# Layout of the first token step's result: 256 adjacent moving elements for the second step, in a state-space convolution kernel

## Chip, cores and metric

The kernel runs on one core of a Trainium2 chip, in one launch. The metric is the time of one execution on the device, in microseconds (us). Three runs of the kernel before gave 220.14, 220.74 and 221.19 us; their median, 220.74 us, is the time before. One more execution was profiled; it took 220.31 us, and its span from the first to the last instruction is 218.5 us.

## What is computed

The reference normalises the input rows, convolves every channel with a long kernel built from the state-space parameters (by FFT over 4096 points), gates the result with a small routed feed-forward network, and adds it to the input:

```
xn = layernorm(A_u)                                   # [1, 2048, 512]
dt = exp(log_dt)
P  = exp(dt * (A_re + i A_im) * l),  l = 0..2047
K  = real(sum_n C[d, n] * P[d, n, l] * dt * B[d, n])  # [512, 2048]
y  = irfft(rfft(pad(xn^T)) * rfft(pad(K)))[:2048]^T + xn * Dskip
r  = xn @ w_r;  row i = argmax(r)
moe = xn, with y_i * sigmoid(r_i) added to row i,
      y_i = (silu(xn_i @ w_gate) * (xn_i @ w_up)) @ w_down
out = A_u + y * silu(moe)
```

The operands are bfloat16.

## The kernel before, in words

The transform over tokens is done with matmuls, in two steps for the input and again for the kernel's spectrum and the way back. The program first writes down a graph of some 925 operations; each carries the SBUF bytes and PSUM banks that it reads and writes, and from these the semaphore waits are derived (`_Graph.op`, `emit`). The order on each engine is a table written out by hand (`ORDER`, applied in `schedule`). Every engine executes its list in order: an instruction that waits holds up all that stands behind it on its engine. The table also fixes which of the PSUM copies run on ScalarE and which on VectorE (`evac`, lines 614 and 615). SyncE's list (SP) holds nearly all DMA issues, so a DMA whose wait is not over holds up the DMAs behind it.

The stages around the change, in the order of time:

- **Norm and router** (`norm`, `new`, `nap`, `nmv`, `rt`, `rarg`). X0 and the parameters' staging tile STG lie in SBUF region RA; the normalised rows XN are moved by DMA into XZN, so that 32 partitions by four quarters hold the tokens.
- **First token step** (`useq`): 16 blocks of four matmuls of 128x256 (moving operand CB's F1, 256 adjacent elements), each into a pair of PSUM banks of 1024 floats. One copy per block (`evac`) writes 1024 bfloat16 per partition into AU, which lies in RA over X0 and STG. ORDER puts 11 of the 16 copies on ScalarE, 5 on VectorE.
- **Second token step** (`useq2`): the table F2U comes by two DMAs into the space that XZN leaves. 16 blocks (one for each pair of frequencies k2) of eight matmuls: stationary operand F2U, 64 rows by 128 columns; moving operand 256 elements of AU on 64 partitions. Two matmuls with `tile_position` (0, 0) and (64, 0) work on the upper and the lower 64 rows of the array at the same time, and write to different PSUM banks; this is a pair below. Each block has four pairs, and alternates between two PSUM bank pairs. A copy on ScalarE takes each block's 1024 floats per partition into one of two UST buffers; after two blocks a buffer goes to DRAM (`scr_u`), from where `load_u` later fetches it, turned, as UU.
- **Beside the second step** ScalarE makes the sines (tile QQ, line 581) and VectorE the products from which the convolution kernel is built: `kgen_g` (tiles TT and GG) and `kgen_q` (QQ). In the table the copies UST stand between groups of four sine instructions. `kgen_mm`, `kgen_kx` (matmuls of QQ with GG, copies KE, KS, KX) turn them into the kernel's points; the small copy K2R on VectorE waits for KX. PE's list mixes the blocks of the second step with the matmuls of the routed network (weights in the ring WRING, vectors in SMB), whose middle is one ScalarE silu and one VectorE product on SMB.
- **Then** the spectrum (`spec`: table FD, loaded in four pieces over RA, that is over AU and WRING; copies KF; product UU), the way back (`inv_a`: copies C) and the last step with the gate (`fin`: TB, XR, stores).

Before the change AU is laid out `[64, 4, 32, 2]`: token group m, quarter a, frequency k2, real or imaginary. The two lines that the change turns around are 879, the copy, and 892, the moving operand:

```
evac(AU(AU.a[4 * m4:4 * m4 + 4].reshape(1024)), pair(pair.a))
lst.append((o_, F2U(...), AU(AU.a[:, :, k2, ri].transpose(1, 0), 64 * par, 64), ...
```

So each copy reads 1024 adjacent floats and writes 1024 adjacent bfloat16, while one moving operand is made of 64 elements 512 bytes apart, four times.

Of the kernel before, what the change touches and what calls it, by code (L numbers as in the profile page):

```python
# [10 lines left out]
BF16 = mybir.dt.bfloat16  # L11
# [398 lines left out]
def build(nc, A_u, A_A_re, A_A_im, A_B_re, A_B_im, A_C_re, A_C_im, A_log_dt, A_Dskip,  # L410
          B_x, B_w_r, B_w_gate, B_w_up, B_w_down, out):
    g = _Graph(nc)
# [54 lines left out]
    with g.ctx:  # L467
# [29 lines left out]
        RA = o + -o % 32  # L497
# [11 lines left out]
        def cb(nm):  # L509
            a, n = cbo[nm]  # L510
            return CB.a[a:a + n]
# [7 lines left out]
        X0 = g.buf("X0", RA, [16, 512], BF16)  # L519
        STG = g.buf("STG", RA + 16 * KB, [6, 4, 128], BF16)  # L520
        ST6 = g.buf("ST6", RA + 22 * KB, [16, 6], F32)
        AU = g.buf("AU", RA, [64, 4, 32, 2], BF16)
        WRING = [g.buf(f"WRING{i}", RA + 32 * KB + 1536 * i, [768], BF16) for i in range(5)]
        FD = g.buf("FD", RA, [32, 5, 128], BF16)
        XN = g.buf("XN", RB, [4, 2, 16, 64], BF16)
# [9 lines left out]
        F2U = g.buf("F2U", RC, [32, 192], BF16)  # L535
# [32 lines left out]
        def cost(eng, v, rate):  # L568
            return FIX[eng] + v.n * rate
# [43 lines left out]
        def evac(out, in_):  # L613
            g.op(AC, lambda e: e.activation(out=out.ap, in_=in_.ap, func=ACT.Copy), w=[out], r=[in_], cost=cost(AC, out, 0.834) - 43,  # L614
                 alt=(DV, lambda e: e.tensor_copy(out=out.ap, in_=in_.ap), cost(DV, out, 1.042)))  # L615
# [10 lines left out]
        def mm(lst, ns):  # L626


            def fn(e):
                for o_, l_, r_, st, sp, pos in lst:  # L630
                    kw = {} if pos is None else {"tile_position": pos}
                    if sp is None:
                        kw["skip_group_check"] = True
                        sp = True
                    ins = e.matmul(o_.ap, lhsT=l_.ap, rhs=r_.ap, start=st, stop=sp, **kw)  # L635
                return ins

            outs, rds, so, sr = [], [], set(), set()
            for o_, l_, r_, _, _, _ in lst:
                k = (o_.banks[0], o_.p0 // 32, (o_.p0 + o_.pn - 1) // 32)  # L640
                if k not in so:
                    so.add(k)
                    outs.append(o_)
                for x in (l_, r_):
                    k = (id(x.buf), x.p0, x.pn, x.idx.tobytes())
                    if k not in sr:
                        sr.add(k)
                        rds.append(x)
            g.op(PE, fn, w=outs, r=rds, cost=ns * len(lst))
# [8 lines left out]
        def store(dst, src, nbytes, eng=SP, tokr=(), tokw=(), w=()):  # L658
            dma(dst, src.ap, nbytes, w=w, r=[src], eng=eng, tokr=tokr, tokw=tokw)

        def dram(t, off, dims):
            return bass.AP(tensor=t, offset=off, ap=dims)
# [112 lines left out]
        for bp in range(8):  # L775
            g.stage = f"rt{bp // 4}"
            pr_, xt = PP[2 * (bp % 2)], XT[bp % 3]
            lst = []
# [51 lines left out]
        for dc in range(4):  # L830
            for wi in range(2):
                W = (B_w_gate, B_w_up)[wi]
                for hf, (f0, fn_) in enumerate(((0, 6), (6, 5))):
# [7 lines left out]
                    lst = [(mv(140, 32), CB(cb("IDB")), gu, True, False, None)] if first else []  # L841
                    for fc in range(f0, f0 + fn_):
                        Mf = 128 if fc < 10 else 96
                        o_ = 128 * (fc - f0)
# [31 lines left out]
        for m4 in range(16):  # L876
            pair = PP[1 + m4 % 2]
            mm([(pair(pair.a[256 * i:256 * i + 256]), XZN(XZN.a[:, :, 4 * m4 + i].reshape(128)), CB(cb("F1")), True, True, None) for i in range(4)], 107)
            evac(AU(AU.a[4 * m4:4 * m4 + 4].reshape(1024)), pair(pair.a))
        g.stage = "ldf2"  # L880
        for k in range(2):
            load(F2U(F2U.a[16 * k:16 * k + 16].reshape(-1)), t_f2u.ap()[:, 3072 * k:3072 * k + 3072], 128 * 6144)
# [1 line left out]
        for kp in range(16):  # L884
            pair = PP[1 + kp % 2]
            lst = []
            for kk in range(2):
                k2 = 2 * kp + kk
                for ri in range(2):
                    for par in range(2):  # L890
                        o_ = pair(pair.a.reshape(2, 4, 2, 2, 32)[par, :, :, kk])
                        lst.append((o_, F2U(F2U.a[k2, 64 - 64 * ri:192 - 64 * ri], 64 * par, 64), AU(AU.a[:, :, k2, ri].transpose(1, 0), 64 * par, 64),
                                    ri == 0, ri == 1, (64 * par, 0)))
            mm(lst, 50)
            st = UST[(kp // 2) % 2]
            j_ = 2 * (kp % 2)
            evac(st(st.a.reshape(2, 8, 128)[:, :, 32 * j_:32 * j_ + 64].transpose(1, 0, 2)), pair(pair.a.reshape(8, 2, 64)))
            if kp % 2:
                store(dram(SCRU, 256 * (kp // 2), [[16384, 128], [2048, 8], [1, 256]]), st(st.a.reshape(8, 256)), 128 * 4096, tokw=[f"scru{kp // 2}"])
# [280 lines left out]
def bass_recurrent_scan__ssm_conv_s4__moe_arch_mod__prompt_kernel(  # L1180
    nc: bass.Bass,
    A_u: bass.AP,
    A_A_re: bass.AP,
    A_A_im: bass.AP,
    A_B_re: bass.AP,
    A_B_im: bass.AP,
    A_C_re: bass.AP,
    A_C_im: bass.AP,
    A_log_dt: bass.AP,
    A_Dskip: bass.AP,  # L1190
    B_x: bass.AP,
    B_w_r: bass.AP,
    B_w_gate: bass.AP,
    B_w_up: bass.AP,
    B_w_down: bass.AP,
    out: bass.AP,
):
    build(nc, A_u, A_A_re, A_A_im, A_B_re, A_B_im, A_C_re, A_C_im, A_log_dt, A_Dskip,
          B_x, B_w_r, B_w_gate, B_w_up, B_w_down, out)
# [28 lines left out]
```

## Time and profile before

| | before |
|---|---|
| median of three runs | 220.74 us |
| the profiled execution | 220.31 us |
| its span | 218.5 us |
| PE busy (matmul) | 157.5 us, 72% |
| VectorE (DVE) busy | 176.9 us, 81% |
| ScalarE (ACT) busy | 143.1 us, 65% |
| mean granted TensorE clock | 0.823 |

Times in the profile are microseconds from the span's start, durations of one instruction are also given in nanoseconds. PE is the matmul, PEld the load of a stationary operand beside it, DVE is VectorE, ACT ScalarE, SPq SyncE's queue of DMA issues. `L614` is line 614. `AU,F2U` behind an arrow are the tiles that an instruction reads; `x128` counts instructions. A row of the timeline gives start, length, engine, line, operation, tiles and count, and in brackets how long the engine had been idle and whose end released it; a row may merge several instructions in a row. A row of groups gives busy time in us, the mean of one in ns, then the idle time before them with the releasers. PEclk is the share of TensorE's full clock that was granted. Matmuls are pipelined: the length of one is the time from its start until its result is there, so the pace of a row of matmuls is read from the distance of their starts. A wait for several semaphores is put down to the one that came last by the profile.

### The profile page before, as it was taken

The page shows a single profiled execution, that of the slowest core. Times are in us where ns is not written, and L with a number is a line of the kernel's source. Part 1 is how long each engine was busy: PE and PEld are TensorE (multiplying, and loading weights), DVE is VectorE, ACT ScalarE, POOL GpSimd, SP SyncE. Part 2 cuts the span into 40 slices and gives each one's busy share as a digit, 9 for nine tenths or more (in the row PEclk, how much of TensorE's full clock was granted, in tenths as well). Part 3 has the DMA queues.
Part 4 walks back from the last instruction along what each step waited for, and adds up shares of the span by engine and source line. Part 5 has one row for each costly group of instructions (what it writes and reads, how often), then busy time and mean ns, then how long its engine had stood idle before and what let it go on. Part 6 is the DMA issues. An engine that isn't in the chain of part 4 may idle for free.

```text
span 218.5 us, 6289 instructions
## 1 busy us (share of the span) xinstructions
PE 157.5 (72%) x2707; PEld 116.9 (54%) x2707; DVE 176.9 (81%) x371; ACT 143.1 (65%) x225; POOL 4.2 (2%) x8
## 2 busy tenths in 40 slices
PE   0300768276728799998988699799976999978650
PEld 0300656144622233632366489698975999967530
DVE  1799999969999479559579997899955799959882
ACT  3599999969995784234141352349947299887670
POOL 0000000001200000000000000300000000000000
PEclk9999997559975555585559999999999799997885
DMA  6920079980076746667289999149198599992577
GB/s 202 338 98 1 2 172 220 177 339 3 0 231 253 214 138 173 180 174 202 60 305 325 357 361 226 37 98 249 47 257 204 96 349 248 204 181 42 94 124 141
DMA packets 37567, 38.90 MB, mean 178 GB/s; under 512 B 10820, under 2 KB 29604, under 8 KB 37156
## 3 DMA queue, kind: packets, MB, share of 16 engines
q1 hardware_dynamic: 34836, 37.46, 64.9%
q10 hardware_dynamic: 2640, 1.04, 2.0%
q8 instruction: 21, 0.34, 0.7%
q14 instruction: 6, 0.05, 0.1%
q0 software_dynamic: 64, 0.00, 0.0%
HBM read 28.01 MB, written 8.39 MB: 167 GB/s over the span
## 4 chain that ended last, share of the span: by engine, by line
PE 56%; DVE 20%; ACT 8%; DMA 5%; issue 5%; SPq 4%; DVEq 0%
PE PB L635 56%; SPq L652 4%; DMA X<-in_A_u_dram 3%; DVE ST L729 3%; DMA XZN<-XN 2%; DVE XN L753 2%; ACT C L614 2%; DVE AU L615 2%; DVE TT L586 1%; ACT AU L614 1%; DVE XR L586 1%; DVE TB L586 1%; DVE UU L586 1%; DVE PAR L586 1%; ACT KF L614 1%
## 5 line engine op out<-in xcount | busy, mean ns | idle before, releaser
L635 PE MATMUL PB<-KX,FD 128*128 128x128 bf16 x640 | 40.4, 221 | 1.6 <-ACT KF L614 1.2
L635 PEld LDWEIGHTS PB<-KX,FD 128*128 128x128 bf16 x640 | 36.7, 99 | 6.1 <-issue 3.3
L635 PE MATMUL PB<-AU,F2U 64*128 64x256 bf16 x128 | 29.4, 602 | 6.3 <-DVE GG L586 4.6
L586 DVE TENSOR_TENSOR TT<-GG,MB 128x512 bf16<-128x512 bf16 (+4 forms) x48 | 30.3, 664 | 0.4
L614 ACT ACTIVATE C<-PB 64x512 bf16<-64x512 f32 x43 | 25.2, 591 | 6.9 <-PE PB L635 4.6
L614 ACT ACTIVATE KF<-PB 128x512 bf16<-128x512 f32 x26 | 15.3, 596 | 22.1 <-PE PB L635 18.4
L614 ACT ACTIVATE UST<-PB 128x1024 bf16<-128x1024 f32 x16 | 16.2, 1026 | 15.7 <-PE PB L635 15.7
L586 DVE TENSOR_TENSOR UU<-UU,KF 128x1024 bf16<-128x1024 bf16 x32 | 21.2, 684 | 5.1 <-ACT C L614 2.6
L635 PE MATMUL PB<-QQ,GG 128*24 128x32 bf16 x1024 | 21.4, 252 | 4.3 <-issue 3.5
L635 PE MATMUL PB<-CB,UU 128*128 128x128 bf16 x256 | 20.9, 240 | 4.1 <-issue 2.2
L635 PEld LDWEIGHTS PB<-QQ,GG 128*24 128x24 bf16 x1024 | 18.5, 134 | 7.4 <-issue 4.4
L635 PEld LDWEIGHTS PB<-CB,UU 128*128 128x128 bf16 x256 | 18.9, 152 | 5.1 <-issue 2.5
L635 PE MATMUL PB<-CB,XN 128*64 128x128 bf16 x128 | 7.5, 297 | 17.1 <-DVE XN L753 15.0
L615 DVE CAST C<-PB 64x512 bf16<-64x512 f32 x21 | 14.4, 687 | 6.1 <-PE PB L635 4.0
L586 DVE TENSOR_TENSOR GG<-TT 128x256 bf16<-128x256 bf16 (+4 forms) x48 | 17.9, 407 | 0.4
L581 ACT ACTIVATE QQ<-TH 128x512 bf16<-128x512 f32 x32 | 18.1, 630 | 0.0
L581 ACT ACTIVATE QQ<-AR 128x512 bf16<-128x512 f32 x33 | 18.1, 614 | 0.0
L635 PEld LDWEIGHTS PB<-AU,F2U 64*128 64x128 bf16 x128 | 6.7, 115 | 20.8 <-issue 13.7
L635 PEld LDWEIGHTS PB<-CB,XN 128*64 128x64 bf16 x128 | 6.1, 158 | 17.8 <-DVE XN L753 15.2
L635 PE MATMUL PB<-CB,XZN 128*128 128x256 bf16 x64 | 11.6, 323 | 5.1 <-DMA XZN<-XN 1.6
L729 DVE BATCH_NORM_STATS2 ST<-X 128x6 f32<-128x512 bf16 x16 | 10.3, 680 | 6.1 <-DMA X<-in_A_u_dram 6.1
L586 DVE TENSOR_TENSOR QQ<-QQ 128x2048 bf16<-128x2048 bf16 (+1 forms) x8 | 14.0, 1755 | 0.2
(120 smaller groups left out, 217.6 us busy)
## 6 DMA issues: line engine op xcount, KB each, us to landing
FD<-c_fd SPq DMA_DIRECT2D x4, 1280.0 KB, 8.6
scr_u<-UST SPq DMA_DIRECT2D x8, 512.0 KB, 4.1
UU<-scr_u SPq DMA_DIRECT2D x8, 512.0 KB, 8.0
UU<-scr_u SPq DMA_DIRECT2D x16, 256.0 KB, 7.6
X<-in_A_u_dram SPq DMA_DIRECT2D x4, 512.0 KB, 6.3
XZN<-XN SPq DMA_DIRECT2D x16, 128.0 KB, 4.1
scr_g<-XN SPq DMA_DIRECT2D x4, 512.0 KB, 7.4
G<-scr_g SPq DMA_DIRECT2D x2, 1024.0 KB
```

The source lines that it names most:

```text
L581: g.op(AC, lambda e: e.activation(out=out.ap, in_=in_.ap, func=func, **kw), w=[out], r=r, cost=cost(AC, out, 0.834) - (43 if in_.buf.space ...
L586: g.op(eng, lambda e: e.tensor_tensor(out=out.ap, in0=a.ap, in1=b.ap, op=op), w=[out], r=[a, b], cost=cost(eng, out, rate))
L614: g.op(AC, lambda e: e.activation(out=out.ap, in_=in_.ap, func=ACT.Copy), w=[out], r=[in_], cost=cost(AC, out, 0.834) - 43, alt=(DV, lambd ...
L615: alt=(DV, lambda e: e.tensor_copy(out=out.ap, in_=in_.ap), cost(DV, out, 1.042)))
L635: ins = e.matmul(o_.ap, lhsT=l_.ap, rhs=r_.ap, start=st, stop=sp, **kw)
L652: fn = lambda e: e.dma_start(dst, src)
L729: g.op(DV, lambda e, b=b: e.bn_stats(ST6(ST6.a[b]).ap, X0(X0.a[b]).ap), w=[ST6(ST6.a[b])], r=[X0(X0.a[b])], cost=620)
L753: lambda e, ov=ov, iv=iv, mv_=mv_, rv=rv: e.tensor_scalar(out=ov.ap, in0=iv.ap, scalar1=mv_.ap, scalar2=rv.ap, op0=ALU.subtract, op1=ALU.m ...
```

## The change

AU is laid out `[32, 2, 4, 64]`: frequency, real or imaginary, quarter, token group. The copy of block m4 now reads its 1024 floats in the order (frequency and part, quarter, i), that is with steps of 256 floats, 64 floats and 1 float, and writes 256 runs of 4 adjacent bfloat16 (8 bytes), 128 bytes apart. The moving operand of the second step is 256 adjacent elements. The number, engines and order of the instructions stay, and so do the computation and the bytes. Which bytes of RA each copy writes and each matmul reads is another, so the derived waits of two kinds differ: the first copies now touch all of AU's 32 KB, and a piece of FD overlays the AU of some k2 alone.

```
-        AU = g.buf("AU", RA, [64, 4, 32, 2], BF16)
+        AU = g.buf("AU", RA, [32, 2, 4, 64], BF16)
...
-            evac(AU(AU.a[4 * m4:4 * m4 + 4].reshape(1024)), pair(pair.a))
+            evac(AU(AU.a[:, :, :, 4 * m4:4 * m4 + 4].reshape(64, 4, 4)), pair(pair.a.reshape(4, 4, 64).transpose(2, 1, 0)))
...
-                        lst.append((o_, F2U(F2U.a[k2, 64 - 64 * ri:192 - 64 * ri], 64 * par, 64), AU(AU.a[:, :, k2, ri].transpose(1, 0), 64 * par, 64),
+                        lst.append((o_, F2U(F2U.a[k2, 64 - 64 * ri:192 - 64 * ri], 64 * par, 64), AU(AU.a[k2, ri].reshape(256), 64 * par, 64),
```

## Prediction

> **What bounds the kernel now.** I read the page first, then the stretches from 66 to 112 us in the timeline, and VectorE's waits there.
>
> ```profile
> PE 56%; DVE 20%; ACT 8%; DMA 5%; issue 5%; SPq 4%; DVEq 0%
> ...
> L635 PE MATMUL PB<-AU,F2U 64*128 64x256 bf16 x128 | 29.4, 602 | 6.3 <-DVE GG L586 4.6
> ```
>
> PE carries 56% of the chain that ended last, and the second token step, the 128 matmuls on AU, keeps PE busy for 29.4 us. What paces them shows in the timeline, where the matmuls of one block stand in one row:
>
> ```profile
> 66.58 1.89 PE L635 MATMUL PB<-AU,F2U 64*128 64x256 bf16 x8 [4.57 <-DVE GG L586]
> 76.89 3.61 PE L635 MATMUL PB<-AU,F2U 64*128 64x256 bf16 x16 [1.76 <-ACT UST L614]
> 92.09 5.34 PE L635 MATMUL PB<-AU,F2U 64*128 64x256 bf16 x24
> ...
> 83.30:86.60 3.30, 3.30 (x16) 0.50 0.72 199
> 93.60:96.90 3.30, 3.30 (x18) 1.00 0.73 198
> ...
> 44.55 1.95 PE L635 MATMUL PB<-CB,XZN 128*128 128x256 bf16 x8 [1.62 <-DMA XZN<-XN]
> 46.76 1.10 PE L635 MATMUL PB<-CB,XZN 128*128 128x256 bf16 x4 [0.26 <-ACT AU L614]
> 44.50:49.10 4.60, 3.84 (x16) 2.51 (x16) 0.50 0.86 354
> ```
>
> Eight more matmuls take 3.61 - 1.89 = 1.72 us, four pairs of 0.43 us; the tail behind the last pair is 1.89 - 4 x 0.43 = 0.17 us. The block of 24 runs at the same 0.43 us ((5.34 - 0.17)/12), though the granted clock, which the rows of stretches give behind the busy times, is 1.00 from 93.6 us and 0.50 around 85 us. So the pair is not paced by the array's clock. The first token step also moves 256 elements per matmul, adjacent ones: four more take 1.95 - 1.10 = 0.85 us, 0.21 us each, at a clock of 0.50. A pair on AU therefore takes just twice what its 256 columns need at the low clock, and the difference between the two operands is the order in memory.
>
> This alone doesn't say what it is worth: the matmuls stand between copies on ScalarE and products on VectorE. VectorE waits only three times between 66 and 112 us, and I take these as the accounts in which a gain must show:
>
> ```profile
> DVE SMB L586 <- ACT SMB L581: 4.5, 1, 4.5
> DVE TT L586 <- ACT QQ L581: 4.2, 1, 4.2
> DVE K2R L596 <- ACT KX L614: 3.9, 1, 3.9
> ...
> 110.70:120.00 9.30, 8.28 (x276) 6.64 (x280) 9.09 (x21) 2.27 (x4) 0.00 (x0) 0.82 0.94 316
> ```
>
> After the third, VectorE is busy for 9.09 of 9.30 us (the third busy time in the row): from there it is at work without a break, and what it starts earlier, it hands on.
>
> **The matmuls.** With adjacent elements I price a pair at 0.21 us, the low-clock row of the first step. A block then takes 4 x 0.21 = 0.85 us plus the tail, and saves 1.72 - 0.85 = 0.87 us. That both matmuls of a pair still run at once is not shown for row tiles with adjacent elements; the pairs of column tiles in the last step show two dense streams at once:
>
> ```profile
> 185.09 0.64 PE L635 MATMUL PB<-C,FB 128*64 128x128 bf16 x16
> 185.00:185.70 0.70, 0.70 (x20) 1.00 1.11 243
> 57.71 0.68 PE L635 MATMUL PB<-CB,XZN 128*128 128x256 bf16 x4 [0.32 <-ACT AU L614]
> 50.68 1.12 PE L635 MATMUL PB<-CB,XZN 128*128 128x256 bf16 x8 [0.56 <-DVE AU L615]
> ```
>
> 16 of them take 0.64 us with the tail; one after another, at the 0.11 us per 256 columns of the first step's faster rows ((1.12 - 0.68)/4), they would take 16 x 0.055 + 0.17 = 1.05 us. Bounds for a pair: 0.11 us, if the clock is full, and 0.43 us, if the pair doesn't overlap. I take 0.21 because the clock was at 0.50 in nearly all of this step. The Trainium skill ("TensorE: Matmul & The Clock Gate", Part 1) says that about 3.4 us of sustained matmul work lift the clock from half to full; the row at 93.60 agrees that a lift happens here. By this rule a pair comes to 0.11 us, and the sum below towards its limit of 208.1 us; I count that as part of the forecast's own range.
>
> **First wait, the sines.** Between ScalarE's sine groups stand the copies UST, which wait for the blocks:
>
> ```profile
> 68.50 1.02 ACT L614 ACTIVATE UST<-PB 128x1024 bf16<-128x1024 f32 x1 [1.38 <-PE PB L635]
> 70.58 1.02 ACT L614 ACTIVATE UST<-PB 128x1024 bf16<-128x1024 f32 x1 [1.05 <-PE PB L635]
> 74.90 1.94 ACT L614 ACTIVATE UST<-PB 128x1024 bf16<-128x1024 f32 x2 [1.22 <-PE PB L635]
> 76.72 2.19 ACT L581 ACTIVATE QQ<-TH 128x512 bf16<-128x512 f32 x4
> 77.91 1.22 DVE L586 TENSOR_TENSOR TT<-QQ 128x2048 bf16<-128x2048 bf16 x1 [4.21 <-ACT QQ L581]
> ```
>
> The first block is ready 0.87 us sooner, the second 0.87 us sooner after it, and the third and fourth then wait for ScalarE rather than it for them: 0.87 + 0.87 + 1.22 = 2.96 us. VectorE's wait of 4.21 for the last sine shrinks to 1.25 us, and all behind it moves up by 2.96.
>
> **Second wait, the routed network's product.** ScalarE's silu stands behind the copy of the block that starts at 92.09:
>
> ```profile
> 82.75 0.69 DVE L593 TENSOR_SCALAR QQ<-TT 128x2048 bf16<-128x2048 bf16 x1
> 86.72 1.30 PE L635 MATMUL PB<-QQ,GG 128*24 128x32 bf16 x64
> 94.02 1.02 ACT L614 ACTIVATE UST<-PB 128x1024 bf16<-128x1024 f32 x1 [3.10 <-PE PB L635]
> 94.94 0.21 ACT L581 ACTIVATE SMB<-SMB 128x11 bf16<-128x11 bf16 x1
> 95.18 0.17 DVE L586 TENSOR_TENSOR SMB<-SMB 128x11 bf16<-128x11 bf16 x1 [4.48 <-ACT SMB L581]
> ```
>
> From 76.89 to 86.72 PE has five blocks (5 x 0.87 = 4.35 us) besides the 2.96, and would be at 79.4; but the matmuls at 86.72 need VectorE's QQ, which ended at 83.44 and now at 80.48. So they gain 6.2 us. One more block before 92.09 and that block itself: the copy of 94.02 comes 6.2 + 2 x 0.87 = 7.9 us earlier, the silu ends about 87.2. VectorE gets there at 95.18 - 4.48 - 2.96 = 87.74, so the whole 4.48 us goes. Cover left: 0.5 us.
>
> **Third wait, KX.**
>
> ```profile
> 107.64 1.03 PE L635 MATMUL PB<-CB,KS 128*128 128x128 bf16 x4
> 109.91 0.70 ACT L614 ACTIVATE KX<-PB 128x640 bf16<-128x640 f32 x1 [5.10 <-PE PB L635]
> 110.65 0.28 DVE L596 CAST K2R<-PB 4x128 bf16<-4x128 f32 x1 [3.93 <-ACT KX L614]
> ```
>
> Up to 107.64 PE has two further blocks of the row at 92.09 and three single ones: with 6.2, seven blocks in all give 6.2 + 7 x 0.87 = 12.3 us, so that KX is there at 110.61 - 12.3 = 98.3. VectorE, 2.96 + 4.48 = 7.44 us earlier, comes to K2R at 110.65 - 3.93 - 7.44 = 99.3. The 3.93 us goes too, with 1 us to spare. Thus VectorE is 2.96 + 4.48 + 3.93 = **11.4 us** earlier, and PE's next matmuls, which need KX and VectorE's products alone, can follow. It can't be more than the three waits, 12.6 us.
>
> **The copies AU.** They keep their number and engines. Their new form, 8-byte runs from reads 1 KB apart, stands in no row; the nearest are these:
>
> ```profile
> L614 ACT ACTIVATE AU<-PB 128x1024 bf16<-128x1024 f32 x11 | 10.8, 1026 | 1.8 <-PE PB L635 1.7
> L615 DVE CAST AU<-PB 128x1024 bf16<-128x1024 f32 x5 | 6.1, 1217 | 0.7 <-PE PB L635 0.6
> L614 ACT ACTIVATE C<-PB 64x512 bf16<-64x512 f32 x43 | 25.2, 591 | 6.9 <-PE PB L635 4.6 <-DVE C L615 1.3
> L614 ACT ACTIVATE KF<-PB 128x512 bf16<-128x512 f32 x26 | 15.3, 596 | 22.1 <-PE PB L635 18.4
> L615 DVE CAST C<-PB 64x512 bf16<-64x512 f32 x21 | 14.4, 687 | 6.1 <-PE PB L635 4.0 <-ACT C L614 1.7
> L615 DVE CAST KF<-PB 128x512 bf16<-128x512 f32 x6 | 4.0, 686 | 1.7 <-PE PB L635 1.5
> ```
>
> C reads single floats 512 bytes apart and writes runs of 16 bytes; KF is dense on both sides; they cost the same on both engines. I take nothing, as C is nearest; at the other end stands the factor of two that the scattered reads of AU cost PE, priced under the rivals.
>
> **What moves along.** The first copies must now wait for all readers of X0 and STG; the last of them writes XN and ends before 31 us, 15 us ahead. The first piece of FD no longer waits for the last block:
>
> ```profile
> 30.47 0.33 DVE XN L753
> 107.75 0.38 SPq L652 DMA_DIRECT2D FD<-c_fd  x1
> scr_u<-UST SPq DMA_DIRECT2D x8, 512.0 KB, 4.1
> ```
>
> On SP it stands behind WRING loads that need PE's network matmul just before that block, so it comes 12 us earlier, with the rest. The stores scr_u move with their copies; each needs 4.1 us, and the next copy into that buffer waits for it.
>
> **Sum.** The profiled execution took 220.31 us; 220.31 - 11.4 = 208.9. It lies 0.4 us below the median of 220.74, to which 209.4 belongs. That is the forecast.
>
> **Rivals.**
>
> 1. *Dear copies, slower.* If 8-byte runs cost a copy what scattered reads cost PE, its 1024 elements take twice as long. 512 elements more are 1026 - 596 = 430 ns on ScalarE and 531 on VectorE, so +0.86 and +1.06 us per copy. ScalarE's 11 alone, less its 1.8 us of waits, delay the sines by 7.7 us; all 16 in one chain, as the blocks wait for them in turn, by 14.8. That ends at 217 to 224, in my view 222 us. It decides from a copy of about 1.9 us on ScalarE. Against it: C beside KF. The Trainium skill ("Advanced Engine Details and Errata", PSUM Cachelines) asks for every two consecutive elements to be adjacent and says that any other pattern slows matmuls; by it the new reads should cost, but C's 591 ns beside KF's 596 disagree for copies.
> 2. *The pair does not get faster.* If the two row tiles share one stream, 0.43 us is 2 x 0.21 and stays: 220.7 us. For it: at the low clock the arithmetic fits. Against: the same 0.43 at the full clock, and the column tiles.
> 3. *A store takes the place of the read.* With two UST buffers a pass of four blocks needs two copies (1.94) and a store (4.1): 1.5 us a block, and my walk from 73.9 to 86 us has eight blocks, so that there is no room in it. If stores take 2 us longer, one or two passes come 2 us later each, the cover is 0.5 us, and the second wait keeps 1.5 to 3.5 us: 211 to 213 us.
>
> **Chances.** Forecast 0.70, copies 0.12 (0.09 of it slower by over 0.5%, the rest 213 to 219), unchanged pair 0.08, store 0.10. The range begins at the limit of 12.6 us, 208.1, less the 0.6 us by which the lowest run lies under the median: 207.5. It ends at 214, above the third rival and a copy dearer by 0.3 us; the second rival and most of the first stay outside. Half a per cent, 1.1 us, is what a measurement of this kernel can tell from no change: faster 0.83, same 0.08, slower 0.09.
>
> **What would show it.** Right: pairs of AU 0.21 us apart or less; VectorE's waits for SMB and K2R gone, that for QQ near 1.25 us; AU copies at 1.03 and 1.22 us; the first UU product 11 us earlier. Wrong: AU copies near 1.9 us; pairs still 0.43 apart; ScalarE waiting for DMA scr_u before UST; or all steps right up to 100 us and the gain lost later, on FD or UU loads.

## The result, and the profile after

| | before | after |
|---|---|---|
| median, four runs of each on one chip | 220.81 us | 207.67 us (207.00 to 208.81) |
| ratio, 95% interval | | 0.941 (0.936 to 0.946) |
| the profiled execution, its span | 220.31, 218.5 us | 207.33, 205.5 us |
| PE busy, VectorE busy | 157.5, 176.9 us | 141.1, 177.1 us |
| mean granted TensorE clock | 0.823 | 0.866 |

Ratios and their intervals, here and below, leave out runs that took over 1.5% longer than the fastest of the same kernel on its chip; medians take all. The changed kernel is 13.1 us faster; 209.4 us was forecast. In its page, the chain of work that ended last and the group of the second token step (busy us and mean ns behind the bar) now read:

```profile
PE 32%; DVE 24%; ACT 16%; DMA 12%; SPq 8%; issue 4%
...
L635 PE MATMUL PB<-AU,F2U 64*128 64x256 bf16 x128 | 14.5, 382 | 6.0 <-ACT QQ L581 4.7
```

PE's share of the chain falls from 56% to 32%, VectorE's rises from 20% to 24%. The 128 matmuls take 14.5 us instead of 29.4. The timeline's rows for them show the pace:

```profile
66.59 1.04 PE L635 MATMUL PB<-AU,F2U 64*128 64x256 bf16 x8 [4.72 <-ACT QQ L581]
69.58 1.89 PE L635 MATMUL PB<-AU,F2U 64*128 64x256 bf16 x16
92.54 0.61 PE L635 MATMUL PB<-AU,F2U 64*128 64x256 bf16 x8
```

and two stretches give the granted clock, the number behind the five busy times (0.50 and 1.00 here):

```profile
70.00:74.00 4.00, 1.93 (x21) 1.11 (x19) 3.57 (x7) 4.00 (x7) 0.00 (x0) 0.50 0.85 227
92.00:96.00 4.00, 3.91 (x56) 2.17 (x55) 3.90 (x5) 2.19 (x3) 0.00 (x0) 1.00 0.90 219
```

At the clock of 0.50 eight more matmuls take 1.89 - 1.04 = 0.85 us, 0.21 us a pair. At the full clock a block takes 0.61 us, less the tail of 0.17 us 0.11 us a pair. Before, it was 0.43 us at both clocks. The copies have the same price as before, in the groups of the first token step:

```profile
L614 ACT ACTIVATE AU<-PB 128x1024 bf16<-128x1024 f32 x11 | 10.9, 1024 | 1.8 <-PE PB L635 1.8
L615 DVE CAST AU<-PB 128x1024 bf16<-128x1024 f32 x5 | 6.1, 1221 | 0.4 <-PE PB L635 0.4
```

That is 1024 and 1221 ns; before the change it was 1026 and 1217. Of VectorE's waits, these remain at the places of the three accounts:

```profile
DVE TT L586 <- ACT QQ L581: 1.3, 1, 1.3
DVE SMB L586 <- ACT SMB L581: 0.5, 1, 0.5
```

(by engine, line and what was waited for: us, times, longest). The products behind them, in VectorE's timeline:

```profile
74.89 1.23 DVE L586 TENSOR_TENSOR TT<-QQ 128x2048 bf16<-128x2048 bf16 x1 [1.29 <-ACT QQ L581]
88.23 0.17 DVE L586 TENSOR_TENSOR SMB<-SMB 128x11 bf16<-128x11 bf16 x1 [0.52 <-ACT SMB L581]
99.72 0.27 DVE L596 CAST K2R<-PB 4x128 bf16<-4x128 f32 x1
```

Before the change they stood at 77.91, 95.18 and 110.65 us. VectorE is thus 3.0, 6.95 and 10.93 us earlier, and the third wait is gone.

### The profile page after: what moved, and what is told of

Its sections match the earlier page's. It is cut to its first block, busy times and chain, and to the rows that moved or that the text cites. A ratio compares the mean times of both kernels' runs of the same rounds, so it can differ in the third digit from the quotient of the medians.

```text
span 205.5 us, 6289 instructions
## 1 busy us (share of the span) xinstructions
PE 141.1 (69%) x2707; PEld 116.0 (56%) x2707; DVE 177.1 (86%) x371; ACT 142.6 (69%) x225; POOL 4.2 (2%) x8
## 3 DMA queue, kind: packets, MB, share of 16 engines
q10 hardware_dynamic: 2640, 1.04, 2.1%
## 4 chain that ended last, share of the span: by engine, by line
PE 32%; DVE 24%; ACT 16%; DMA 12%; SPq 8%; issue 4%
PE PB L635 32%; SPq L652 8%; DMA XR<-in_A_u_dram 7%; ACT QQ L581 5%; ACT AU L614 5%; DVE QQ L586 3%; DMA X<-in_A_u_dram 3%; DVE ST L729 3%; DVE TT L586 3%; DMA XZN<-XN 3%; DVE XR L586 2%; DVE XN L753 2%; ACT UST L614 2%; DVE C L615 2%; DVE TB L586 2%
## 5 line engine op out<-in xcount | busy, mean ns | idle before, releaser
L635 PE MATMUL PB<-KX,FD 128*128 128x128 bf16 x640 | 41.0, 223 | 2.1 <-ACT KF L614 1.2
L635 PEld LDWEIGHTS PB<-KX,FD 128*128 128x128 bf16 x640 | 37.3, 100 | 6.7 <-issue 3.9
L635 PE MATMUL PB<-CB,UU 128*128 128x128 bf16 x256 | 19.3, 229 | 3.3 <-issue 2.2
L635 PEld LDWEIGHTS PB<-CB,UU 128*128 128x128 bf16 x256 | 17.5, 150 | 4.3 <-issue 2.3
L635 PE MATMUL PB<-AU,F2U 64*128 64x256 bf16 x128 | 14.5, 382 | 6.0 <-ACT QQ L581 4.7
L635 PEld LDWEIGHTS PB<-AU,F2U 64*128 64x128 bf16 x128 | 7.2, 125 | 10.1 <-DVE GG L586 4.8
```

## Experiments: the copies or the reads

**Reads only.** The copies are the old ones, the operand is 256 adjacent elements:

```
-            evac(AU(AU.a[:, :, :, 4 * m4:4 * m4 + 4].reshape(64, 4, 4)), pair(pair.a.reshape(4, 4, 64).transpose(2, 1, 0)))
+            evac(AU(AU.a.reshape(16, 1024)[m4]), pair(pair.a))
```

> The copies write AU as in the kernel before, 1024 adjacent elements each; the second step's moving operand is 256 adjacent elements at the same addresses as in the changed kernel. The values it reads are therefore in the wrong places: the output is not the reference's, the amount of work is. My theory (the whole gain is in the reads of the second step, the copies' new pattern is free): the time of the changed kernel, 207.7 us within 1 us, AU copies of 1.02 and 1.22 us, pairs of 0.21 us at the low clock and 0.11 us at the full one. Rival (the new write pattern costs something that other gains hide): faster than 207.7 us by over 1 us, with shorter AU copies. Rival (the layout of the writes itself is a part of the gain, by banks of SBUF or by waits on AU): slower than 209 us.

Measured: 209.15 us, ratio to the kernel before on its chip 0.945 (0.934 to 0.957); that chip's runs of the kernel before reached from 218.39 to 224.37 us, hence the wide interval. Copies 1021 and 1222 ns, a block of eight 1.04 us at the low clock. The median is a hair above the second rival's 209 us, and the time alone excludes neither rival. But the copies' own rows leave them nothing to work with, and VectorE reaches K2R at 100.0 us, after 99.7 in the changed kernel: the new write pattern saves and costs nothing that can be read.

**Writes only.** The copies are the new ones, the operand hops 512 bytes again:

```
-  AU(AU.a[k2, ri].reshape(256), 64 * par, 64)
+  AU(AU.a.reshape(64, 4, 32, 2)[:, :, k2, ri].transpose(1, 0), 64 * par, 64)
```

> The copies write AU as in the changed kernel; the moving operand hops 512 bytes from element to element, as in the kernel before, over the same buffer. The values it reads are in the wrong places, the amount of work is unchanged. My theory: the time of the kernel before, 220.8 us within 1 us, pairs of 0.43 us at both clocks, VectorE's three waits (about 4.2, 4.5 and 3.9 us) back. Rival (the copies' pattern is a part of the gain): between 209 and 219 us. Rival (the copies' pattern costs): over 222 us.

Measured: 221.8 us, ratio 1.002 (0.995 to 1.008). VectorE's longest waits at those places:

```profile
DVE SMB L586 <- ACT SMB L581: 4.5, 1, 4.5
DVE K2R L596 <- ACT KX L614: 4.3, 2, 3.9
DVE TT L586 <- ACT QQ L581: 3.7, 1, 3.7
```

and the page's group of the second step:

```profile
L635 PE MATMUL PB<-AU,F2U 64*128 64x256 bf16 x128 | 29.4, 602 | 5.9 <-ACT QQ L581 4.1
```

All three waits are back, and the 29.4 us to the tenth. So the whole gain is in the reads.

## Experiments: what makes a read fast

**The order of the matmuls.** The four matmuls of one row tile first, then the four of the other:

```
-            for kk in range(2):
-                k2 = 2 * kp + kk
-                for ri in range(2):
-                    for par in range(2):
+            for par in range(2):
+                for kk in range(2):
+                    k2 = 2 * kp + kk
+                    for ri in range(2):
```

> The changed kernel with the eight matmuls of a block in another order: the four of one row tile first, then the four of the other, so that only one pair in four has its two row tiles back to back. The result is the same. My theory (the adjacent elements let the two row tiles of a pair stream at the same time at 0.21 us for 256 columns; without alternation each matmul takes that by itself): a block of about 1.7 us at the low clock, as in the kernel before, and about 0.9 us at the full clock. With the clock as low as it was before over these blocks the gain goes, about 219 us; where TensorE, now busy without a gap, is granted the full clock earlier, less is lost, down to 212 us. Rival (the two row tiles did not overlap in the changed kernel either, each matmul of adjacent elements takes 0.11 us at either clock): 207.7 us, unchanged.

Measured: 208.11 us, ratio 0.947 (0.937 to 0.957), and nothing changes in the blocks:

```profile
68.72 1.05 PE L635 MATMUL PB<-AU,F2U 64*128 64x256 bf16 x8
70.49 1.90 PE L635 MATMUL PB<-AU,F2U 64*128 64x256 bf16 x16
92.55 0.62 PE L635 MATMUL PB<-AU,F2U 64*128 64x256 bf16 x8
```

My expectation failed. Either its rival is right, and a matmul of 64 rows takes half the time by itself, or two row tiles run side by side even where their matmuls are issued in fours. This run can't tell; the next one was made for that.

**One row tile alone.** All eight matmuls of a block on partitions 0 to 63, adjacent elements in even blocks, the hop in odd ones:

```
-  F2U(..., 64 * par, 64), AU(AU.a[k2, ri].reshape(256), 64 * par, 64), ..., (64 * par, 0)
+  F2U(..., 0, 64), AU(old_operand if kp % 2 else AU.a[k2, ri].reshape(256), 0, 64), ..., (0, 0)
```

(`old_operand` stands for the operand of the second run.)

> The changed kernel with all eight matmuls of a block on the same row tile, partitions 0 to 63 (so half of the data is left out and the output is not the reference's); in even blocks the moving operand is 256 adjacent elements, in odd blocks it hops 512 bytes as before the change. It measures one row tile's own pace, without the reordering of the third run, in which two row tiles could still run side by side. Adjacent elements, theory (two row tiles stream at the same time): each matmul 0.21 us at the low clock, eight 1.7 us, and 0.11 us at the full clock; rival (each matmul of 64 rows takes half the time): 0.11 us each at the low clock, eight 0.85 us. Hopping elements, theory A (each row tile fetches by itself, one 16 bytes' piece in 1.7 ns): 0.43 us for each matmul, eight 3.4 us; theory B (the two row tiles share one stream of fetches, so that 0.43 us is 2 x 0.21): 0.21 us each, eight 1.7 us.

One execution was measured: 233.09 us. The first odd block and the first even block in the timeline:

```profile
65.32 3.60 PE L635 MATMUL PB<-AU,F2U 64*128 64x256 bf16 x8 [4.14 <-ACT QQ L581]
69.10 1.89 PE L635 MATMUL PB<-AU,F2U 64*128 64x256 bf16 x8
```

and the stretch around them, with its clock of 0.50:

```profile
66.00:70.00 4.00, 4.00 (x18) 1.48 (x17) 3.93 (x6) 1.31 (x2) 0.00 (x0) 0.50 0.55 222
```

Adjacent: (1.89 - 0.17)/8 = 0.215 us each at the low clock. Hopping: (3.60 - 0.17)/8 = 0.43 us each. (The clock stayed at 0.50 up to 110 us, so there is no reading at the full one.) In the changed kernel eight matmuls on two row tiles take 0.85 us, here on one tile 1.72. So two row tiles do run side by side, in the kernel before as well, whether they alternate or come in fours; each fetches its operand by itself, and 0.43 us was one tile's pace, not 2 x 0.21 on a shared stream.

**Every second, fourth, eighth element, and runs of two.** Four runs of one execution each, with the old dense copies; the operand takes every s-th element, or two adjacent ones and then a hop of 512 bytes:

```
-  AU(AU.a[k2, ri].reshape(256), 64 * par, 64)
+  AU(AU.a.reshape(-1)[256 * ((2 * k2 + ri) % (64 - s)):][:256 * s:s], 64 * par, 64)              # s = 2, 4, 8
+  AU(AU.a.reshape(64, 64, 2, 2)[:, 2 * k2 % 64 + ri].transpose(1, 0, 2), 64 * par, 64)           # runs of two
```

> The copies write AU densely as in the kernel before, and the moving operand takes every second element, so 4 bytes from one to the next (values in the wrong places, the same amount of work). Theory A (what counts is how many elements follow each other within 16 bytes, at least two; the Trainium skill says so in Advanced Engine Details and Errata, SBUF Cachelines): four elements to 16 bytes, full pace, pairs of 0.21 us at the low clock, about 207.7 us. Theory B (only elements next to each other are fast): pairs of 0.43 us, about 220 us. Theory C (the pace falls with the bytes spanned): between, pairs of about 0.21 us at the low clock, over 0.11 us at the full clock.

> As the run with every second element, but every fourth, 8 bytes from one to the next. Theory A (two hits within 16 bytes are enough): pairs of 0.21 us at the low clock and 0.11 us at the full one, about 207.7 us. Theory B (only adjacent elements are fast): pairs of 0.43 us, about 220 us. Theory C (the pace falls with the bytes spanned): pairs over 0.21 us and under 0.43 us, between 208 and 220 us.

> As the run with every second element, but every eighth, 16 bytes from one to the next. Theory A (one hit within 16 bytes is too few): pairs of 0.43 us at both clocks, about 220 us. Theory B (only adjacent elements are fast): the same 0.43 us and 220 us. Theory D (short hops are free and the hop of 512 bytes is what cost, by landing in one bank each time): pairs of 0.21 us and about 207.7 us.

> The copies write AU densely as in the kernel before; the moving operand takes two adjacent elements and then hops 512 bytes (values in the wrong places, the same amount of work). Theory A (two elements within the same 16 bytes are enough, however far the hop): pairs of 0.21 us at the low clock and 0.11 us at the full one, about 207.7 us. Theory B (only long runs are fast): pairs over 0.3 us, 215 to 220 us. Theory D (the hop of 512 bytes itself costs, half as often here): pairs of about 0.21 us at both clocks, so about the changed kernel's time at the low clock and slower at the full one.

Measured: 206.82, 206.33, 221.22 and 207.51 us, beside 219.71 us for the kernel before. The rows of the timeline are, for every second element (the last one at a clock of 1.00),

```profile
67.97 1.03 PE L635 MATMUL PB<-AU,F2U 64*128 64x256 bf16 x8
69.73 1.89 PE L635 MATMUL PB<-AU,F2U 64*128 64x256 bf16 x16
92.59 0.63 PE L635 MATMUL PB<-AU,F2U 64*128 64x256 bf16 x8
```

for every fourth

```profile
67.96 1.07 PE L635 MATMUL PB<-AU,F2U 64*128 64x256 bf16 x8
69.75 1.98 PE L635 MATMUL PB<-AU,F2U 64*128 64x256 bf16 x16
92.16 1.07 PE L635 MATMUL PB<-AU,F2U 64*128 64x256 bf16 x8
```

with this stretch, at a clock of 1.00, around the last block,

```profile
92.00:96.00 4.00, 4.00 (x30) 1.43 (x30) 3.90 (x7) 1.82 (x3) 0.00 (x0) 1.00 0.72 173
```

for every eighth

```profile
68.85 1.96 PE L635 MATMUL PB<-AU,F2U 64*128 64x256 bf16 x8
71.53 3.77 PE L635 MATMUL PB<-AU,F2U 64*128 64x256 bf16 x16
```

and for runs of two, where the clock was 1.00 from 89 us on:

```profile
67.24 1.03 PE L635 MATMUL PB<-AU,F2U 64*128 64x256 bf16 x8
69.00 1.90 PE L635 MATMUL PB<-AU,F2U 64*128 64x256 bf16 x16
92.74 1.03 PE L635 MATMUL PB<-AU,F2U 64*128 64x256 bf16 x8
```

With the differences at the low clock, and the block less 0.17 us at the full one, a pair costs:

| operand | 16-byte pieces in 256 elements | clock 0.50 | clock 1.00 |
|---|---|---|---|
| adjacent | 32 | 0.21 us | 0.11 us |
| every second | 64 | 0.21 | 0.115 |
| every fourth | 128 | 0.23 | 0.225 |
| runs of two, hops of 512 bytes | 128 | 0.22 | 0.215 |
| every eighth | 256 | 0.45 | |
| hops of 512 bytes (before) | 256 | 0.43 | 0.43 |

Both columns of prices fit the larger of two: 256 columns at the array's clock (0.21 or 0.11 us), or the number of 16-byte pieces at 1.7 ns each (0.43 us/256), whatever the clock. Theory A holds at the low clock: two elements to a piece are enough, and how far the hop goes does not matter. At the full clock it doesn't: two elements to a piece are half as fast as four. Theory B is refuted by every second element, theory D by every eighth (0.45 us without a long hop), though what D said of runs of two, 0.21 us at both clocks, came true. C is refuted as it was worded: runs of two span far more bytes than every fourth element and cost the same. The Trainium skill ("Advanced Engine Details and Errata", SBUF Cachelines) says that SBUF is read in lines of 16 bytes and that at least two hits on a line are needed to hide the access; the runs agree at a clock of 0.50 and ask for four bfloat16 elements at 1.00. The kernel's time hardly sees the difference, since few of its blocks run at the full clock.

## Experiments: where the gain stops

In the changed kernel's timelines of PE and of ScalarE there are new waits; the one at 99.41 us stands ahead of the first matmuls of the next stage:

```profile
84.91 1.16 PE L635 MATMUL PB<-QQ,GG 128*24 128x32 bf16 x56 [0.99 <-issue]
99.41 1.30 PE L635 MATMUL PB<-QQ,GG 128*24 128x32 bf16 x64 [3.10 <-DVE QQ L593]
103.68 0.49 PE L635 MATMUL PB<-QQ,GG 128*24 128x32 bf16 x17 [0.26 <-issue]
...
78.04 1.02 ACT L614 ACTIVATE UST<-PB 128x1024 bf16<-128x1024 f32 x1 [0.32 <-DMA scr_u<-UST]
81.52 2.14 ACT L614 ACTIVATE UST<-PB 128x1024 bf16<-128x1024 f32 x2 [1.26 <-DMA scr_u<-UST]
87.07 1.02 ACT L614 ACTIVATE UST<-PB 128x1024 bf16<-128x1024 f32 x1 [3.41 <-PE PB L635]
87.99 0.21 ACT L581 ACTIVATE SMB<-SMB 128x11 bf16<-128x11 bf16 x1
```

TensorE now waits 3.10 us for VectorE there: of PE's gain that much has no use. In the seven profiles with fast reads and this order of the engines (the changed kernel twice, the reads only, the other order of the matmuls, every second and every fourth element, runs of two) the stage starts between 98.33 and 99.82 us; in six of them TensorE waits 1.88 to 3.48 us for VectorE, in the run with the reads only 0.88 us for the copy KX. Two changes of order and one added instruction test whether VectorE is the path there.

**Sines and silu earlier.** In the tables of ScalarE and TensorE:

```
- scalar  ... 442 310 312 422 436 439 441 317 315 ... 325 330 238 332 ...
+ scalar  ... 442 310 422 436 439 441 312 315 317 ... 325 238 330 332 ...
- tensor  ... 311 309 225 316 314 227 ...
+ tensor  ... 311 309 225 314 316 227 ...
```

(422, 436, 439 and 441 are the last sines, 238 is the silu; 310, 312, 315, 317 and 330 are copies UST; 314 and 316 are two blocks.)

> The changed kernel with another order on two engines, result the same: ScalarE makes the last four sines ahead of the second copy of the block pair that it stood behind, and the silu ahead of the copy before it; TensorE swaps the two blocks that follow. It aims at what is left of VectorE's waits, 1.29 us for the sines and 0.52 us for the silu. My theory (VectorE's waits in the overlap are the account, and TensorE's first matmuls on its products wait 3.10 us for it): these two waits go, VectorE comes 1.3 to 1.8 us earlier to the first block of the next stage and the time falls by 1.0 to 1.7 us, to about 206.3 us. Rival (from there on TensorE and the transfers bound it, VectorE's work is covered): VectorE is earlier at that place, the time stays within 0.5 us of 207.7 us. Rival (the later copy holds a PSUM bank and TensorE loses what VectorE gains): the wait of TensorE for the UST copy grows by over 1 us, and the time does not fall.

Measured: 207.51 us, ratio 0.935 (0.925 to 0.945). The two waits are gone but for 0.10 us, and in PE's timeline:

```profile
98.06 1.30 PE L635 MATMUL PB<-QQ,GG 128*24 128x32 bf16 x64 [2.11 <-DVE QQ L593]
103.15 0.50 PE L635 MATMUL PB<-QQ,GG 128*24 128x32 bf16 x17 [1.09 <-issue]
```

The stage starts 1.35 us earlier; 0.83 us of it is lost in the stop put down to issue, which was 0.26 us in the one profile of the changed kernel. Whether that stop is larger by this order or by chance, and what the time does, needed both kernels on one chip again. First the changed kernel:

> The changed kernel once more, unaltered, so that the next two can be compared with it on the same chip: 0.94 of the kernel before, 207 to 209 us where that takes 220 to 221 us.

Measured: 208.49 us (206.98 to 210.05), ratio 0.941 (0.936 to 0.946). In its own profile the stop is 0.98 us, and in the other five of the seven 0.70 to 2.06 us, so the 0.26 was luck:

```profile
98.73 1.30 PE L635 MATMUL PB<-QQ,GG 128*24 128x32 bf16 x64 [2.89 <-DVE QQ L593]
103.73 0.50 PE L635 MATMUL PB<-QQ,GG 128*24 128x32 bf16 x17 [0.98 <-issue]
```

And beside it the other order again:

> The order of engines tried before (the last sines and the silu earlier), again beside the changed kernel. In its first profile VectorE came 1.35 us earlier to the first matmuls of the next stage and TensorE's wait there fell from 3.10 to 2.11 us, but a stop of TensorE's own a few us later, which the profile puts down to issue, was 1.09 us where it was 0.26 us in the changed kernel's profile. My theory (VectorE's account is the path there): 1.0 to 1.5 us under the changed kernel on this chip, in the profile the two waits gone again. Rival (what VectorE gains there is lost to the issue stops and the transfers later): within 0.5 us of it.

Measured: 207.51 us (206.27 to 209.90), ratio 0.938 (0.933 to 0.942). That is 0.98 us less than the changed kernel, just under the theory's range of 1.0 to 1.5 us, and the intervals overlap: the time leaves it open. In the profile both waits are gone again (0.15 us is left) and the stage starts at 98.18 us, 0.55 us ahead of the changed kernel's profile on this chip, as that one had come earlier itself (waits of 0.8 and 0.2 us for sines and silu). The gain is there up to this place; that it reaches the end is not shown.

**One more VectorE instruction.** A maximum over 2048 elements, ahead of the product on SMB (in `tt`, at operation 518):

```
+  e.tensor_reduce(out=SCR().ap, in_=MB(MB.a[0:2].reshape(2048)).ap, axis=AX.X, op=ALU.max)
   e.tensor_tensor(out=out.ap, in0=a.ap, in1=b.ap, op=op)
```

> The changed kernel with one more VectorE instruction in the overlap, ahead of its wait for the silu: a maximum over 2048 elements of MB, which nobody reads, some 2.2 us by the 1.3 ns an element of its slowest operations on 512 elements. The result is the same. In the kernel before this place had 4.5 us to spare. My theory (after the change VectorE binds here and TensorE waits for it): 0.52 us of it goes into the wait for the silu, the rest arrives whole: the first matmuls of the next stage start 1.6 to 1.8 us later and the kernel takes 1.5 to 1.9 us more than the changed one, about 209.4 us. Rival (TensorE and the transfers bind again behind that place and swallow it): under 0.7 us more.

Measured: 209.70 us (208.33 to 210.41), ratio 0.947 (0.943 to 0.951): 1.2 us over the changed kernel, between the theory's range and the rival's bound. In VectorE's and PE's timelines:

```profile
86.70 2.29 DVE L586 TENSOR_REDUCE SCR<-MB 128x1 f32<-128x2048 bf16 x1
90.05 0.15 DVE L586 TENSOR_TENSOR SMB<-SMB 128x11 bf16<-128x11 bf16 x1
101.19 1.30 PE L635 MATMUL PB<-QQ,GG 128*24 128x32 bf16 x64 [4.80 <-DVE QQ L593]
102.69 3.08 PE L635 MATMUL PB<-QQ,GG 128*24 128x32 bf16 x122
```

The added instruction took 2.29 us, and no wait for the silu is left. The stage starts 101.19 - 99.41 = 1.78 us later than in the changed kernel's first profile, which the theory was drawn from (1.6 to 1.8 us), but 2.46 us later than in the profile beside it, where the wait for the silu was only 0.19 us. The stop for issue within the stage is gone. A reading of this is that the stop passes while TensorE waits for VectorE, so that the two are not lost twice; no run tests it. The 1.2 us do not decide it either, since the intervals of the two ratios (0.943 to 0.951 and 0.936 to 0.946) just overlap. So VectorE is the path up to this stage, as TensorE's waits for it show; how much of what is won or lost on it reaches the end stays open.

## Why the prediction was right

**The pair, 0.21 us.** Right, and for the stated reason: two row tiles run side by side (one tile alone takes 1.72 us for eight). Its second rival, a shared stream, is refuted by the same run. Towards the end the pair is at 0.11 us, as the forecast's own lower limit had it.

**The first wait, 4.21 to 1.25 us.** 1.29 us.

**The second wait, 4.48 to 0.** 0.52 us stayed. The silu was put at 87.2 us and ended at 88.2: PE had a stop for issue of 0.99 us (the row at 84.91) ahead of the block that the copy at 87.07 waits for, and the walk had no room for it. The seven profiles bear this out: a stop there of 0.65 to 1.03 us goes with a wait for the silu of 0.19 to 0.52 us in four of them, and in the three where it is at most 0.10 us VectorE does not wait. ScalarE also waits 0.32 and 1.26 us for stores scr_u before its copies, the sign that the prediction gave for its third rival. They cost the silu nothing: ScalarE then idles for 3.41 us until PE's block is there. The price of 4.1 us a store was right (4.2 us in the page).

**The third wait, 3.93 to 0.** Right, in part by the clock's favour. KX was put at 98.3 us and ended at 97.04, since the last three blocks (92.54 us and behind it) ran at the full clock. In the run with the reads only, the clock was 0.50 from 93 to 97 us, they took 1.03 us each, KX ended at 99.59 us, and VectorE came to K2R at 100.04: little of the 1 us to spare was left. The sum of the three, 11.4 us, measured 10.93 at K2R in the two profiles on record. Over more profiles: with the slow reads (the kernel before, and the run with the new writes alone) VectorE reaches K2R at 110.6 and 110.9 us; in the seven profiles with fast reads at 98.6 to 100.1, on average 99.5. That is 11.3 us. (Every eighth element, slow as well at 0.45 us a pair, has 112.05.)

**"From there it is at work without a break, and what it starts earlier, it hands on."** This step held for what was handed on and missed what came on top: the end moved by 13.0 us in the profiles and 13.1 in the medians, more than the 12.6 us that the prediction called the most. The first UU product comes 10.92 us earlier (at 117.79 us, before at 128.71), as was said. The additional wait stands behind the end of the stretches I read, at the fifth UU product. In the timeline of the kernel before, SyncE's issues of two FD loads, of the last store of scr_u and of the loads UU that wait for it, and VectorE's product:

```profile
115.01 1.03 SPq L652 DMA_DIRECT2D FD<-c_fd  x2
116.09 0.57 SPq L652 DMA_DIRECT2D scr_u<-UST  x1
127.08 1.68 SPq L652 DMA_DIRECT2D UU<-scr_u  x3
...
135.54 0.69 DVE L586 TENSOR_TENSOR UU<-UU,KF 128x1024 bf16<-128x1024 bf16 x1 [1.16 <-DMA UU<-scr_u]
```

and the same in the changed kernel:

```profile
102.88 0.98 SPq L652 DMA_DIRECT2D FD<-c_fd  x2
103.90 0.57 SPq L652 DMA_DIRECT2D scr_u<-UST  x1
114.61 1.68 SPq L652 DMA_DIRECT2D UU<-scr_u  x3
...
123.11 0.67 DVE L586 TENSOR_TENSOR UU<-UU,KF 128x1024 bf16<-128x1024 bf16 x1
```

The last store needs 11 us to land in both kernels, where the median store takes 4.1 and 4.2 us, and the loads wait for it. It is issued right behind two FD loads; whether they hold it up, no run here tests. It is issued 12.2 us earlier, the loads 12.5 us earlier: ahead of it on SyncE's list stand a store that waits for a copy UST and WRING loads that wait for TensorE's network matmuls, so it does not move with VectorE alone. VectorE, itself 10.9 us earlier, no longer waits for the loads: the 1.16 us goes, and the UU product at 123.11 is 12.43 us earlier. With the new writes alone this wait is 2.09 us, in the seven profiles with fast reads 0 in six and 0.63 in one. From K2R to this product VectorE takes 24.89, 26.02 and 25.10 us with slow reads (the kernel before, the new writes alone, every eighth element), and 23.38 to 24.38 us in the seven: 1.6 us less on average. From there to the end of the span it is 82.25 to 83.04 us and 81.22 to 85.81 us, which shows no further gain. So what the prediction had wrong here is the number of accounts: there were four, and 11.4 + 1.2 = 12.6 would have given 208.1 us. The half us left over is within these differences between profiles.

**The number.** 207.67 us lies 1.7 us under the forecast, and under 208.1 us, the limit that the prediction set for its own sum. The range holds it only by the 0.6 us that was taken off for the scatter of the runs, so that part is luck.

**"PE's next matmuls can follow."** They do, but not with all that PE gains: they wait 3.10 us for VectorE (the row at 99.41). In the sum this cost nothing, since it went by VectorE's account.

**The copies at no cost.** Right, and shown by both halves of the change. The rule of the Trainium skill ("Advanced Engine Details and Errata", PSUM Cachelines) that the prediction's first rival draws on names matmuls, and no copy here bears it out: reads 1 KB apart in PSUM and 8-byte writes cost the same 1.02 and 1.22 us.

**What moves along.** The first FD load is issued at 95.19 us, 12.6 us earlier, after the last AU block (94.28 + 0.61 = 94.89 us): the wait that the change loosened was not used.

## What to carry to other kernels

Look at what paces a matmul: where its time did not follow the granted clock here, it was fed too slowly, and the order of its moving operand in SBUF was the cause. Two bfloat16 elements in each 16-byte piece were enough at the low clock, four at the full one, and the copy that writes the operand did the reordering free of charge (1.02 and 1.22 us, as before). What a faster engine is worth is read from the waits of the engine that waits for it, one after another until the next common point, and the list must not end with the stage: here a fourth wait, for transfers behind it, went as well, since they came earlier by more (12.5 us) than the engine that waits for them (10.9 us). A rearrangement that takes a wait away may be given back in a stop for issue nearby, so one profile does not settle a microsecond.

## What was not expected of the hardware

- Two row tiles run side by side even when four matmuls of the one are issued before the four of the other (1.04 and 1.05 us a block in the two orders, 1.89 on one tile).
- The prices of all six operand orders fit a fetch in 16-byte pieces at about 1.7 ns each for one row tile, at both granted clocks (0.43 to 0.45 us for 256 pieces, 0.215 to 0.23 us for 128).
- With the slow operand the full clock came later, though PE was busier. With hops of 512 bytes PE was busy 4.00 of 4.00 us from 82 to 86 us at a clock of 0.50, and of 0.50 still from 96 to 99 us, in the run with the new writes alone; with adjacent elements PE was busy 3.01 of those 4 us and the clock was 0.93 there. By which measure the clock is granted, no run here tells.
